# An mLSTM cell and a mixture of depths on one core: stores moved behind the loads, gates loaded later, fillers removed, gathers started sooner

## The chip, the core and the metric

The kernel runs on one core of a Trainium2 chip. The core has five engines with a queue of instructions each: TensorE (PE, matrix products), VectorE (DVE), ScalarE (ACT), GpSimd (POOL) and SyncE (SP, which only starts transfers here), and 16 DMA engines that all transfers share. Every engine works through its own queue in order and waits on semaphores for the others. The metric is the device time of one execution in microseconds. Lower is better. The kernel before takes 215.62 us, the median of 3 runs (212.85 to 220.34); the profiled execution has a span of 216.6 us.

## The reference

Two blocks follow each other. The first is an mLSTM cell for 4 batches, 8 heads, 768 positions and head size 40:

```python
for t in range(S):
    m_new  = np.maximum(f_gate[:, :, t] + m, i_gate[:, :, t])
    f_stab = np.exp(f_gate[:, :, t] + m - m_new)
    i_stab = np.exp(i_gate[:, :, t] - m_new)
    C = f_stab * C + i_stab * outer(v_t, k_t)
    n = f_stab * n + i_stab * k_t
    y[:, :, t] = sigmoid(o_gate[:, :, t]) * (C @ q_t) / max(|n . q_t|, 1)
```

The result is brought to x of shape (4, 768, 320). The second block is a mixture of depths: for each batch the scores `x @ w_gate` are ranked, the 128 highest of the 768 rows are picked, and only these get a layer:

```python
    top = argpartition(-scores[b], 128)[:128]
    h = relu(x[b, top] @ w1)              # 320 -> 1024
    out[b, top] = x[b, top] + sigmoid(scores[b, top])[:, None] * (h @ w2)
```

All other rows of the output are x itself.

## The kernel before

The recurrence is computed in blocks. One step n of the main loop (12 steps, `for n in range(N)`) handles 256 positions of one batch, all 8 heads; `b, s = divmod(n, 3)`, so each batch has the steps s = 0, 1, 2. The 256 positions are held as 128 partitions times c = 2, and the states are taken every 64 positions.

What one step does: `scores` (k times q, L260), `masked` (VectorE applies the causal mask, giving P), `update` (k times the weighted v for the next step, L227, into pU), `states` (VectorE adds up the states C), `widen` (ScalarE copies q into a padded tile), `weigh` (POOL multiplies v by the gates, giving wv, L213), `turn` (transposes of k and q on TensorE, L201, copied back by ScalarE, L203 and L205), `read` (q times the states, L282, into pH), `attend` (P times wv added into pH, L292), `divide` (VectorE normalizes, giving y, L301 to L306), `sigmoid` (ScalarE, on the output gates o), `output` (POOL multiplies y by o, giving x, L314), `store` (x to the output in DRAM), `router` (VectorE, the product of x with w_gate, L329). Update, turn, widen and weigh work ahead of their step: in step n they handle n+1 or n+2.

The second block of batch b-1 runs inside the steps of batch b: `spread` (L357, each score broadcast to all partitions; s = 0), `ranks` (each row counts the scores above its own, half of the rows on VectorE with L367, half on ScalarE by signs with L372), `select` (L404, a 0/1 matrix from ranks), `fetch` (L444, which products yield the indices of the picked rows; then POOL starts a gather from the output in DRAM, L446), `fetched` (transposes of the gathered rows, L454, and xeT on ScalarE, L456), `layer1` (L471, two halves) and `layer2` (L480, then yg on ScalarE, L485, and a scatter that adds onto the output, L486). The last batch has no gather: `picked` forms its rows by products with the selection (L428). At the end `good` says whether two assumptions held; each engine reads it into a register (L590), and a general version of the kernel, `_general`, runs only if they did not.

Order: `_fast` runs under a manual schedule, so the order of the lines of the program is the order in each engine's queue. A wait in a queue holds up everything behind it in that queue. Three tiles each (NB) hold k, q and v, four (NO) hold the output gates, two serve each use of PSUM tag "t", which turns, index products and layers share, and one holds pU, pH, and pS or pB.

Loads: `load(n + 3)` at the top of step n starts four transfers for v and k, one for q and four for o, on SyncE. The four o transfers go into the tile that `output(n - 1)` reads last. Each transfer waits for the one eight places before it to land, over SyncE's and ScalarE's transfers together, since eight semaphores serve in turn. Stores are started by ScalarE. The weights w1 and w2 are loaded in steps 1 and 2.

Fillers: `fill(k)` multiplies a tile of ones k times into a PSUM tile that nobody reads (L495), to keep TensorE at work.

Of the kernel before, what the change touches and what calls it, by code (L numbers as in the profile page):

```python
# [26 lines left out]
def _fast(ctx, tc, q, k, v, i_gate, f_gate, o_gate, w_gate, w1_in, w2_in, out):  # L27


    nc = tc.nc  # L30
# [8 lines left out]
    WARM = 14  # L39
# [19 lines left out]
    def load(n):  # L59
        if n >= N:  # L60
            return
        b, s = divmod(n, NS)
        for t, src in ((v_t, v), (k_t, k)):
            for c in range(2):
                a = s * 256 + c * 128
                SP.dma_start(out=t[n % NB][:, c, :, 0:D], in_=src[b, :, a:a + 128, :].rearrange("h p d -> p h d"))
        SP.dma_start(out=q_t[n % NB], in_=q[b, :, 256 * s:256 * s + 256, :].rearrange("h (p t) d -> p h (t d)", t=2))
        for r in range(2):
            for c in range(2):
                a = s * 256 + c * 128 + r * 64  # L70
                SP.dma_start(out=o_t[n % NO][64 * c:64 * c + 64, r], in_=o_gate[b, :, a:a + 64, :].rearrange("h p d -> p h d"))  # L71
# [19 lines left out]
    ident = const.tile([128, 128], FP, name="ident")  # L91
    for i in range(NB):
        POOL.memset(k_t[i][:, :, :, D:DP], 0.0)
        POOL.memset(v_t[i][:, :, :, D:D1], 1.0)
        if i == 0:
            make_identity(nc, ident)
        if i < 2:
            POOL.memset(qw_t[i][:, :, :, D:DP], 0.0)
        if i == 0:
            POOL.memset(wv_t[0], 0.0)  # L100
# [5 lines left out]
    ind = gate.tile([BH, 2, 64], FP, name="ind")  # L106
    DVE.tensor_copy(out=ind, in_=odd.unsqueeze(2).to_broadcast([BH, 2, 64]))
# [42 lines left out]
    def gate_rows(s):  # L150
        own = slice(256 * s, 256 * s + 256)
        carry = m[:, s:s + 1]
        F = gate.tile([BH, 256], FP, name="F", tag="F")
        a = gate.tile([BH, 256], FP, name="a", tag="a")
        M = gate.tile([BH, 256], FP, name="M", tag="M")
        Me = gate.tile([BH, 2], FP, name="Me", tag="Me")
        E = gate.tile([BH, 514], FP, name=f"E{s}")
        DVE.tensor_tensor_scan(out=F, data0=one, data1=f_sb[:, own], initial=0.0, op0=OP.mult, op1=OP.add)
        DVE.tensor_tensor(out=a, in0=i_sb[:, own], in1=F, op=OP.subtract)
        DVE.tensor_tensor_scan(out=M, data0=one, data1=a, initial=carry, op0=OP.mult, op1=OP.max)  # L160
        DVE.tensor_scalar(out=Me[:, 1:2], in0=M[:, 255:256], scalar1=-1.0, scalar2=None, op0=OP.mult)
        DVE.tensor_scalar(out=E[:, 256:512], in0=a, scalar1=M[:, 255:256], scalar2=None, op0=OP.subtract)
        DVE.tensor_tensor(out=E[:, 512:513], in0=carry, in1=M[:, 255:256], op=OP.subtract)
        DVE.tensor_scalar(out=E[:, 0:256].rearrange("b (r c t) -> b c r t", r=2, c=2),
                          in0=M.rearrange("b (c r t) -> b c r t", c=2, r=2), scalar1=M[:, 255:256], scalar2=None,
                          op0=OP.subtract)
        DVE.tensor_tensor(out=m[:, s + 1:s + 2], in0=F[:, 255:256], in1=M[:, 255:256], op=OP.add)
        ACT.activation(out=E[:, 0:513], in_=E[:, 0:513], func=AF.Exp)
        rowed[s] = E

    def gate_cols(s):
        E = rowed[s]
        dz = gate.tile([BH, 128], FP, name=f"dz{s}")
        DVE.tensor_scalar(out=dz, in0=ind.rearrange("b j e -> b (j e)"), scalar1=E[:, 512:513], scalar2=None, op0=OP.mult)
# [56 lines left out]
    def states(n):  # L231

        for i in range(4):
# [83 lines left out]
    def store(n):  # L317
        b, s = divmod(n, NS)
        for c in range(2):
            a = 256 * s + 128 * c  # L320
            ACT.dma_start(out=out[b, a:a + 128, :].rearrange("(r t) d -> t r d", t=64),
                          in_=x_t[b % 2][64 * c:64 * c + 64, 2 * s:2 * s + 2, 0:DM])
# [95 lines left out]
    def picked(b):  # L418
# [7 lines left out]
        for r in range(2 * NS):  # L426
            for j in range(3):
                PE.matmul(pX[:, j, :], x[:, r, 128 * j:128 * j + 128], sel[:, r, :],  # L428
                          start=(r == 0 and j == 0), stop=(r == 2 * NS - 1), skip_group_check=True)
        d["xeT"] = mod.tile([128, 3, 128], FP, name="xeT")  # L430
        ACT.copy(out=d["xeT"], in_=pX)
# [6 lines left out]
    def fetch(b):  # L438

        d = dep[b]  # L440
        sel = d["sel"]
        pi = ps_t.tile([128, 3], FP, name="pi", tag="t")
        for r in range(2 * NS):
            PE.matmul(pi, sel[:, r, :], place[:, r, :], start=(r == 0), stop=(r == 2 * NS - 1))  # L444
        index(b, pi[:, 0:1], pi[:, 1:2], pi[:, 2:3])
        POOL.indirect_dma_start(out=xe_t[b % 2][:, 0:DM], out_offset=None, in_=out[0:b + 1].rearrange("b s d -> (b s) d"),  # L446
                                in_offset=bass.IndirectOffsetOnAxis(ap=d["idx"], axis=0),
                                bounds_check=(b + 1) * S - 1, oob_is_err=False)
# [42 lines left out]
    def fill(k):  # L491

        pf = ps_t.tile([128, 512], FP, name="pf", tag="t")
        for i in range(k):
            PE.matmul(pf[:, 128 * (i % 4):128 * (i % 4) + 128], hot, hot, start=True, stop=True)  # L495

    gate_rows(0)
    causal()
    gate_cols(0)
    weigh(0)  # L500
    POOL.memset(wv_t[1], 0.0)
    tables()
    margins()
    turn(0, "kT")
    widen(0)
    update(0)
    turn(0, "qT")
    scores(0)
    gate_rows(1)
    gate_rows(2)  # L510
    fill(6)
    gate_cols(1)
    gate_cols(2)
    weigh(1)
    POOL.memset(wv_t[2], 0.0)
    states(0)
    for n in range(N):
# [3 lines left out]
        if n == 1:  # L521
# [3 lines left out]
        if n == 2:  # L525
            SP.dma_start(out=w2, in_=w2_in.rearrange("(f p) d -> p f d", p=128))
        if n > 0:
            scores(n)
        masked(n)
        if n < NS:  # L530
            fill(6)
        if more:
            update(n + 1)
            states(n + 1)
        sigmoid(n)
        if more:
            widen(n + 1)
        if n + 2 < N:
            weigh(n + 2)
        if n > 0:  # L540
            router(n - 1)
        if b > 0 and s == 1:
            select(b - 1)
        if more:
            turn(n + 1, "kT")
        if n < 5 or n == 7:
            fill(4)
        if b > 0 and s == 2:
            fetched(b - 1)
            layer1(b - 1, 0)  # L550
            layer1(b - 1, 4)
        if b > 1 and s == 0:
            layer2(b - 2)
        read(n)
        if more:
            turn(n + 1, "qT")
            if b > 0 and s == 0:
                dep[b - 1] = {"sb": spread(b - 1, 0, 2 * NS)}
        else:
            gated(n)  # L560
# [6 lines left out]
        if n > 0:  # L567
            store(n - 1)
        if b > 0 and s == 0:
            ranks(b - 1)  # L570
        if b > 0 and s == 1:
            fetch(b - 1)
# [3 lines left out]
    layer2(b - 1, 0, 4)  # L576
    ranks_last(b)
    store(N - 1)
    layer2(b - 1, 4)
    fill(8)  # L580
    picked(b)
    good = gate.tile([1, 1], I32, name="good")
    pg = ps_t.tile([1, NS + B], FP, name="pg", tag="t")
# [4 lines left out]
    layer1(b, 0)  # L588
    layer1(b, 4)
# [354 lines left out]
```

## Time and profile before

| what | value |
|---|---|
| median of 3 runs | 215.62 us |
| span of the profiled execution | 216.6 us |
| busy: PE, DVE, ACT, POOL | 173.7, 101.6, 73.5, 74.4 us |
| mean granted TensorE clock | 0.887 of full |
| fillers (L495), busy | 17.6 us, 112 records (each product of 32-bit numbers has two) |
| transfers | 24.33 MB, 112 GB/s over the span |

Where each step's scores begin, in us from the start of the span (TensorE's timeline, L260):

| step | 0 | 1 | 2 | 3 | 4 | 5 | 6 | 7 | 8 | 9 | 10 | 11 |
|---|---|---|---|---|---|---|---|---|---|---|---|---|
| us | 15.84 | 31.35 | 41.07 | 52.02 | 67.57 | 77.44 | 96.72 | 109.70 | 121.17 | 143.06 | 156.04 | 165.11 |

The page of the profile gives, per engine, the busy time and, in 40 slices of the span, the busy share, the clock granted to TensorE and the share of the DMA engines, each in tenths as one digit. Its chain follows the work that ended last back to what released it, and so says which engine or transfer set the end. A wait is listed with the one who waited, whom it waited for, the total, the number of times and the longest. In the tables by stage each engine has its busy time with the number of instructions in brackets, then come the clock, the DMA share and GB/s. In timelines a line is: start, length, engine, line, operation, written tile <- read tiles, sizes, count, and in square brackets the idle time before it with its releaser. "PEld" is the load of weights, "SPq" and "ACTq" are the queues that issue transfers. Busy time of an engine that nobody waits for costs nothing.

### The profile page before, as it was taken

How to read it: one execution, taken by the hardware profiler on the slowest of the kernel's cores; microseconds unless marked ns; L12 is line 12 of the kernel's file. 1: busy time of each engine (PE TensorE's matmuls, PEld its weight loads, DVE VectorE, ACT ScalarE, POOL GpSimd, SP SyncE). 2: the span in 40 equal slices, each digit the busy share in tenths (PEclk: the TensorE clock that was granted, in tenths of full speed). 3: DMA queues.
4: the chain of work that ended last, by engine and by line, in shares of the span. 5: the costliest groups of instructions: out<-in, count | busy, mean ns of one | idle time of the engine just before them, and what ended most of it. 6: DMA issues, size and time to landing. Idle time of an engine off the chain costs nothing.

```text
span 216.6 us, 6856 instructions
## 1 busy us (share of the span) xinstructions
PE 173.7 (80%) x2961; PEld 154.2 (71%) x2961; DVE 101.6 (47%) x273; ACT 73.5 (34%) x134; POOL 74.4 (34%) x95
## 2 busy tenths in 40 slices
PE   7477999899499691999997908999984299997960
PEld 7366898788499681997877808996974199696940
DVE  7795727364444974019168660056199200831000
ACT  2425141424116551143384411242592103811200
POOL 8495707070421636007243343025232500320011
PEclk9969799999959999799997975899999559998895
DMA  5999999939989789955989991020312100240002
GB/s 113 174 160 166 184 142 163 200 60 271 181 184 275 129 170 178 157 96 99 181 162 184 175 205 18 0 67 0 58 39 64 30 0 3 62 87 9 5 9 33
DMA packets 93608, 24.33 MB, mean 112 GB/s; under 512 B 88352, under 2 KB 93088, under 8 KB 93568
## 3 DMA queue, kind: packets, MB, share of 16 engines
q1 hardware_dynamic: 89392, 18.72, 51.1%
q10 hardware_dynamic: 3456, 3.93, 6.8%
q0 software_dynamic: 720, 1.15, 3.5%
q8 instruction: 25, 0.41, 0.8%
q14 instruction: 15, 0.12, 0.2%
HBM read 19.20 MB, written 4.59 MB: 110 GB/s over the span
## 4 chain that ended last, share of the span: by engine, by line
PE 45%; DMA 15%; issue 12%; SPq 7%; DVE 6%; POOL 5%; ACT 5%; ACTq 1%; POOLq 0%
PE ph L471 11%; PE pf L495 6%; DMA xe<-out_dram,idx 6%; PE pt L201 5%; SPq L71 5%; PE py L480 4%; PE pH L282 4%; PE pH L292 4%; PE pU L227 4%; DMA o<-in_o_gate_dram 3%; DMA out_dram<-x 3%; DMA v<-in_v_dram 3%; POOL wv L213 2%; PE pS L260 2%; PE pX L428 2%
## 5 line engine op out<-in xcount | busy, mean ns | idle before, releaser
L314 POOL TENSOR_TENSOR x<-y,o 128x320 f32<-128x320 f32 x24 | 20.5, 874 | 93.9 <-DVE y L306 23.3
L213 POOL TENSOR_TENSOR wv<-v,cols 64x656 f32<-64x656 f32 x24 | 31.8, 1326 | 14.3 <-DVE cols L182 5.7
L301 DVE SCALAR_TENSOR_TENSOR den<-pH,cols 128x16 f32<-128x16 f32 x12 | 2.1, 174 | 66.9 <-PE pH L292 66.9
L471 PE MATMUL ph<-xeT,w 128*128 128x128 f32 x192 | 30.7, 337 | 1.7 <-ACT xeT L456 1.7
L471 PEld LDWEIGHTS ph<-xeT,w 128*128 128x128 f32 x192 | 29.9, 251 | 2.8 <-ACT xeT L456 2.7
L205 ACT COPY qT<-pt 128x512 f32<-128x512 f32 x24 | 13.9, 629 | 26.6 <-PE pt L201 26.6
L203 ACT COPY kT<-pt 128x512 f32<-128x512 f32 x24 | 12.9, 586 | 26.8 <-PE pt L201 26.7
L227 PE MATMUL pU<-wv,k 128*64 128x82 f32 x384 | 17.8, 248 | 4.7 <-issue 2.6
L495 PE MATMUL pf<-hot 128*128 128x128 f32 x112 | 17.6, 311 | 4.5 <-ACT kT L203 4.5
L495 PEld LDWEIGHTS pf<-hot 128*128 128x128 f32 x112 | 15.4, 216 | 6.3 <-ACT kT L203 5.9
L227 PEld LDWEIGHTS pU<-wv,k 128*64 128x64 f32 x384 | 15.6, 145 | 6.1 <-issue 3.0
L480 PE MATMUL py<-w,hT 128*128 128x320 f32 x64 | 18.4, 437 | 0.6 <-ACT kT L203 0.6
L292 PE MATMUL pH<-wv,P 128*64 128x82 f32 x384 | 16.7, 239 | 0.0
L292 PEld LDWEIGHTS pH<-wv,P 128*64 128x64 f32 x384 | 14.7, 138 | 2.0 <-issue 1.3
L329 DVE CUSTOM_DVE_ANT_0 scr<-x,wg 128x320 f32<-128x320 f32 x22 | 15.2, 691 | 1.6
L239 DVE TENSOR_TENSOR C<-pU,C 128x164 f32<-128x164 f32 x40 | 13.1, 327 | 5.9 <-PE pU L227 4.8
L486 POOL DMA_INDIRECT out_dram<-yg,idx x4 | 6.3, 1584 | 27.4 <-ACT yg L485 23.7
L480 PEld LDWEIGHTS py<-w,hT 128*128 128x128 f32 x64 | 11.8, 190 | 5.4 <-ACT kT L203 1.1
L201 PE MATMUL pt<-ident,qw 128*128 128x128 f32 x96 | 15.1, 307 | 0.6 <-ACT kT L203 0.6
L260 PE MATMUL pS<-qT,kT 40*64 40x64 f32 x768 | 14.3, 221 | 1.6 <-issue 0.9
L266 DVE TENSOR_TENSOR P<-pS,mask 128x1024 f32<-128x1024 f32 x12 | 14.6, 1214 | 0.7 <-PE pS L260 0.7
L282 PEld LDWEIGHTS pH<-C,qT 40*64 40x64 f32 x704 | 13.3, 143 | 2.2 <-issue 1.3
(110 smaller groups left out, 240.6 us busy)
## 6 DMA issues: line engine op xcount, KB each, us to landing
v<-in_v_dram SPq DMA_DIRECT2D x24, 160.0 KB, 4.4
k<-in_k_dram SPq DMA_DIRECT2D x24, 160.0 KB, 4.4
q<-in_q_dram SPq DMA_DIRECT2D x12, 320.0 KB, 5.8
o<-in_o_gate_dram SPq DMA_DIRECT2D x48, 80.0 KB, 4.3
out_dram<-x ACTq DMA_DIRECT2D x24, 160.0 KB, 3.6
w<-in_moe_w_dram SPq DMA_DIRECT2D x1, 1280.0 KB
w<-in_moe_w_dram SPq DMA_DIRECT2D x2, 512.0 KB, 5.7
w<-in_moe_w_dram SPq DMA_DIRECT2D x1, 256.0 KB
```

Source lines behind the costliest of these rows:

```text
L201: PE.transpose(pt[:, p, :], src[:, c, 2 * p:2 * p + 2, :].rearrange("s j d -> s (j d)"), ident)
L213: POOL.tensor_tensor(out=wv_t[n % 3][o, :, :, r], in0=v_t[n % NB][o], op=OP.mult, in1=cols[s][o, 0:2, b * H:b * H + H].unsqueeze(3).to_bro ...
L227: PE.matmul(pU[64 * j:64 * j + 64, c, p], k_t[n % NB][:, c, 2 * p + j, :], wv_t[n % 3][:, c, 2 * p + j], start=True, stop=True)
L260: PE.matmul(pS[o, j, c, p, :], kT[e, p, t], qT[e, p, t], start=True, stop=True)
L266: DVE.tensor_tensor(out=P.rearrange(flat), in0=pending[n].pop("pS").rearrange(flat), op=OP.mult, in1=mask.unsqueeze(1).to_broadcast([128, ...
L282: PE.matmul(g["pH"][64 * c:64 * c + 64, NP * j + p, r], g["qT"][e, p, t], state[n, 2 * c + r][e, p, :], start=(c, j) not in g["begun"], st ...
L292: PE.matmul(g["pH"][64 * c:64 * c + 64, NP * j + p], g["P"][:, j, c, p, :], wv_t[n % 3][:, c, 2 * p + j], start=(c, j) not in g["begun"], ...
L314: POOL.tensor_tensor(out=x.rearrange(order, j=2, d=D), in0=pending[n]["y"][:, r].rearrange("s (j p) d -> s j p d", j=2), in1=o.rearrange(o ...
L329: DVE.tensor_tensor_reduce(out=scr, in0=x[:, r, 0:DM], in1=wg, scale=1.0, scalar=0.0, op0=OP.mult, op1=OP.add, accum_out=x[:, r, DM:DM + 1])
L471: PE.matmul(ph[:, f, :], w1[:, j, (f0 + f) * 128:(f0 + f) * 128 + 128], d["xeT"][:, j, :], start=(j == 0), stop=(j == 2))
L480: PE.matmul(d["py"], d["hT"][:, f, :], w2[:, f, :], start=(f == 0), stop=(f == NF - 1))
L495: PE.matmul(pf[:, 128 * (i % 4):128 * (i % 4) + 128], hot, hot, start=True, stop=True)
```

## The change

Five things are changed in `_fast`. Stores are started by SyncE, behind the loads of the same step, instead of by ScalarE. The output gates are loaded one step later than q, k and v. No fillers are left, and 18 instead of 14 products run at the very start. For the gathers, ranks, selection and the index products move ahead inside the s = 1 steps, and the gather stands before POOL's `output`; layer 2 of a batch moves to the s = 1 steps, where it runs before the update, and layer 1 behind the turn of q. In the tail the layers of the last two batches follow each other: the third batch's rows, its layer 1 (in halves, with the ranking of the last batch between) and layer 2, then the last batch's. The start is rearranged as well: most zeroing moves from POOL to ScalarE, the gate rows are split in two, and the gates of steps 1 and 2 are computed in step order, one each in the start and in step 0. The purpose is to let TensorE go on with useful work, to let loads run ahead of TensorE and to have the gathered rows there when layer 1 wants them.

```diff
-    WARM = 14
+    WARM = 18
     def load(n):
...
+        if n < N:
+            b, s = divmod(n, NS)
...
+        n -= 1
+        if 0 <= n < N:
...
+                SP.dma_start(out=o_t[n % NO][64 * c:64 * c + 64, r],
+                                 in_=o_gate[b, :, a:a + 64, :].rearrange("h p d -> p h d"))
...
+    def zero(t):
+        shape = [128, 2, H, t.shape[-1]]
+        ACT.activation(out=t, in_=hot[:, 0:1].unsqueeze(2).unsqueeze(3).to_broadcast(shape), func=AF.Copy, scale=0.0)
...
     def store(n):
...
-            ACT.dma_start(out=out[b, a:a + 128, :].rearrange("(r t) d -> t r d", t=64),
+            SP.dma_start(out=out[b, a:a + 128, :].rearrange("(r t) d -> t r d", t=64),
...
     def picked(b):
-        for r in range(2 * NS):
-            for j in range(3):
-                PE.matmul(pX[:, j, :], x[:, r, 128 * j:128 * j + 128], sel[:, r, :],
-                          start=(r == 0 and j == 0), stop=(r == 2 * NS - 1), skip_group_check=True)
-        ACT.copy(out=d["xeT"], in_=pX)
+        for j in range(3):
+            for r in range(2 * NS):
+                PE.matmul(pX[:, j, :], x[:, r, 128 * j:128 * j + 128], sel[:, r, :], start=(r == 0), stop=(r == 2 * NS - 1))
+            ACT.copy(out=d["xeT"][:, j], in_=pX[:, j])
...
+    gate_sums(0)
     gate_rows(0)
+    gate_sums(1)
     causal()
     gate_cols(0)
     weigh(0)
...
     turn(0, "kT")
+    gate_rows(1)
     widen(0)
     update(0)
     turn(0, "qT")
+    gate_cols(1)
+    weigh(1)
+    gate_sums(2)
     scores(0)
-    gate_rows(1)
-    gate_rows(2)
-    fill(6)
-    gate_cols(1)
-    gate_cols(2)
-    weigh(1)
-    states(0)
     for n in range(N):
         load(n + 3)
-        if n == 1:
+        if n == 3:
 ...
-        if n == 2:
+        if n == 4:
 ...
         if n > 0:
+            store(n - 1)
+        if n > 0:
             scores(n)
         masked(n)
-        if n < NS:
-            fill(6)
+        if n == 0:
+            states(0)
+            gate_rows(2)
+        if b > 1 and s == 1:
+            layer2(b - 2)
+        if n > 0 and (s < 2 or not more):
+            router(n - 1)
+        if b > 0 and s == 1:
+            ranks(b - 1)
+            select(b - 1)
         if more:
             update(n + 1)
-            states(n + 1)
-        sigmoid(n)
-        if more:
+            states(n + 1, 0, 4 if n else 3)
             widen(n + 1)
...
-        if n < 5 or n == 7:
-            fill(4)
-        if b > 0 and s == 2:
-            fetched(b - 1)
-            layer1(b - 1, 0)
-            layer1(b - 1, 4)
-        if b > 1 and s == 0:
-            layer2(b - 2)
         read(n)
+        if b > 0 and s == 1:
+            numbers(b - 1)
+            fetch(b - 1)
+        if n == 0:
+            gate_cols(2)
+            states(1, 3)
+            weigh(2)
+            tables()
         if more:
             turn(n + 1, "qT")
+            sigmoid(n)
             if b > 0 and s == 0:
                 dep[b - 1] = {"sb": spread(b - 1, 0, 2 * NS)}
+            if b > 0 and s == 2:
+                fetched(b - 1)
+                layer1(b - 1, 0)
+                layer1(b - 1, 4)
...
-        if n > 0:
-            store(n - 1)
-        if b > 0 and s == 0:
-            ranks(b - 1)
-        if b > 0 and s == 1:
-            fetch(b - 1)
...
     output(N - 1)
-    layer2(b - 1, 0, 4)
+    fetched(b - 1)
+    layer1(b - 1, 0)
     ranks_last(b)
     store(N - 1)
-    layer2(b - 1, 4)
-    fill(8)
+    layer1(b - 1, 4)
+    layer2(b - 1)
     picked(b)
     layer1(b, 0)
     layer1(b, 4)
+    picked_numbers(b)
     layer2(b)
```

`numbers` is the first half of what `fetch` was (the index products and VectorE's arithmetic on them), `picked_numbers` the last lines of what `picked` was.

## The prediction

> **What bounds the kernel now.** I read the page's slices first (its rows for the granted TensorE clock and for the DMA), then its chain, then the table of waits, the busy time by stage, and TensorE's timeline. A "step" n below is one block of 256 rows, and begins when its scores (L260) begin.
>
> ```profile
> PEclk9969799999959999799997975899999559998895
> DMA  5999999939989789955989991020312100240002
> ```
>
> One slice is 5.4 us. The DMA engines are full until slice 23 (about 126 us) and nearly idle afterwards; the matmul clock is low in some six places. So two thirds of the kernel run beside a full DMA, and the last third has none to blame.
>
> ```profile
> PE 45%; DMA 15%; issue 12%; SPq 7%; DVE 6%; POOL 5%; ACT 5%; ACTq 1%; POOLq 0%
> ```
>
> The chain is mostly TensorE. What stops it (who waits <- for whom: us in total, times, longest), with the load queue's own waits in the last two lines:
>
> ```profile
> PE pX L454 <- DMA xe<-out_dram,idx: 14.9, 3, 5.3
> SPq L71 <- DMA out_dram<-x: 12.0, 3, 7.1
> SPq L66 <- DMA out_dram<-x: 12.0, 4, 6.6
> ```
>
> Three gathers of picked rows cost TensorE 14.9 us, and loads on SyncE wait 24 us behind stores. By stage (steps 1 and 5 of 0 to 11):
>
> ```profile
> 31.40:41.10 9.70, 9.46 (x234) 8.51 (x232) 5.48 (x12) 2.93 (x6) 4.22 (x4) 1.00 1.10 165
> 77.40:96.70 19.30, 14.34 (x264) 13.29 (x260) 5.89 (x20) 5.35 (x10) 5.84 (x5) 0.91 0.90 155
> ```
>
> In step 1 TensorE is busy 9.46 of 9.70 us, but 2.7 of that are fillers; in step 5 it is idle 5 us. The timeline shows both kinds of loss:
>
> ```profile
> 32.44 1.60 PE L495 MATMUL pf<-hot 128*128 128x128 f32 x12
> 56.71 0.64 PE L227 MATMUL pU<-wv,k 128*64 128x82 f32 x11 [2.61 <-issue]
> 62.54 1.97 PE L201 MATMUL pt<-ident,qw 128*128 128x128 f32 x8
> 85.31 0.52 PE L454 MATMUL pX<-ident,xe 128*128 128x128 f32 x3 [4.39 <-DMA xe<-out_dram,idx]
> 86.39 7.00 PE L471 MATMUL ph<-xeT,w 128*128 128x128 f32 x48 [0.57 <-ACT xeT L456]
> ```
>
> The transposes of 62.54 take 1.97 us where others take 1.09: half clock, after the gap of 2.61 us.
>
> [...]loads move at 165 GB/s while slices with weights reach 271.
>
> **Prices**, start to start at full clock: scores 1.1, update 1.3, k turn 1.05, read 1.07, q turn 1.03, attend 1.3: a plain step needs 6.8 us of TensorE. The score broadcast (L357) adds 1.4, layer 1 7.0, layer 2 4.5.
>
> **Part by part.**
>
> Costed at nothing: the 18 instead of 14 warming products lie in the wait for the first gates (TensorE idles 1.6 us before 7.46); the constants made later on POOL stand beside TensorE's turns; the picked rows copied in thirds save 0.2 us, in the tail's sum.
>
> Fillers out: 56 products, 17.6 us busy, nearly all in line on TensorE. They lie in the start and in steps 0 to 4 and 7 (about 15 us) and in the tail (1.9, partly beside the ranking).
>
> Start: the zeroing goes to ScalarE[...] the first gates are ready at 5.4, since the 2.5 us of "ind" are gone: nothing lost, scores(0) at 14.8 instead of 15.8. Step 0 held 15.5 us: both further gate rows, a DVE-to-PE round trip, two fillers. In the new order only gates 2 stand in it: 6.8 + 0.8 of transposes + about 2 of waiting for POOL's wv(1) (2.6 us after cols(1)) = 9.7.
>
> Output gates later: each load set is 0.98 MB of q, k, v, then 0.33 MB of gates of the step before. They need not wait for output(n-1) (POOL), and k, v, q arrive 2 us sooner. At 165 GB/s, with 1.2 us per pair of stores and about 4.4 us each for w1 and w2 (their slices run at 271 GB/s), set n has landed at about 16, 23, 31, 39, 48, 57, 69, 83, 92, 101, 110 us (n = 1 to 11; each is the one before plus 1.31 MB at 165 GB/s = 7.9 us, plus the 1.2 us of the stores from set 5 on, plus 4.4 us for w1 ahead of set 7 and w2 ahead of set 8). TensorE needs set n+1 at 1.1 us into step n. By the sums below it arrives just in time for steps 1 to 4, and early afterwards.
>
> Stores behind loads: ScalarE loses 24 issues of 0.62 us, 1.2 us a step, which lay beside TensorE: nothing gained directly. A store now waits on SyncE for output(n-1), 3.5 us into step n; behind it stand the loads of n+4, whose buffers come free only about 4 us into step n: no loss. But store(2) stands behind load 6, gates 5 and w1, so it lands near 65 us, and the first gather needs it.
>
> Steps with s=1 (4, 7, 10): ranks, selection and indices are pulled up. VectorE: mask until 2.95 us after the step's start, router until 4.1 (POOL's second x), three comparisons of 1.07, selection 0.95: 8.4. TensorE reaches the index product (L444 of before) at 4.5 and stands for 3.9 us; the second q turn then waits for its PSUM buffer until VectorE has made the states (1.4) and the indices (0.5), 10.4. Step 4 takes 12.2 us against 7.05 of work. In steps 7 and 10 layer 2 (4.5) fills that hole, but its ScalarE output stands ahead of the three sign passes (3.3 us), so selection ends at 10.6: 14.4 us.
>
> Steps with s=2 (5, 8): indices were ready 11.7 us into step 4, now 10.4, and layer 1 moves behind the q turn, 5.5 us into the next step. From index to landed rows took 6.0 us in step 4 of before (79.3 to 85.3), of which 1.7 waited for POOL's multiplication (L314), behind which the gather no longer stands; about 4.5 is left, and the rows are there: the stalls of 4.4, 5.3 and 5.2 us go. Left is 1.5 us for sigmoid and xeT copy. 6.8 + 0.5 + 7.0 + 1.5 = 15.8. Step 5 alone waits for store(2): rows at 69 us, TensorE there at 65: +4.2.
>
> Steps with s=0 (3, 6, 9): 8.5 (6.8 + 1.4 + gaps). Layer 2 leaves 6 and 9.
>
> Sum: 14.8 start; 9.7, 7.2, 7.5, 8.5, 12.2, 20.0, 8.5, 14.4, 15.8, 8.5, 14.4 = 126.7 for steps 0 to 10 (before: 149.3).
>
> Tail from scores(11): scores, read, broadcast after router(10), attend 6.4; transposes 0.6; xeT behind four sign passes 2.9; layer 1 in halves with the broadcast of the last rows 7.6; layer 2 4.5; picked rows 4.3 and last copy 0.3; layer 1 7.0; then index product, indices, flags, "good" and its register load (0.48 us, now between layers on TensorE) 2.3; layer 2 4.5; scatter to the end as before 7.3: 47.8 (before 51.5).
>
> 14.8 + 126.7 + 47.8 = 189. This is at full clock with no issue gaps. Before, TensorE's busy 173.7 us stands against 162.6 by my prices, so 11 us went to the low clock, in five or six places; the new order also has five gaps of 1.8 us or more. I add 10: **199 us**. With half of that and no store wait: 190.
>
> **Rivals.** (a) The transfers eat the gain: stores queue behind loads at each batch, gathers stall three times by 5 us, sets arrive late. 199 + 12 = 211. For it: DMA near 1.0 until 126 us, so the floor for the last set is 110 to 118. Against: after step 5 TensorE needs longer per step than the 9 us of DMA. (b) No change: the waits in s=1 steps are 5 us longer than I think and the clock falls in each: 199 + 3 x 6 = 217. (c) Slower: without fillers TensorE works 6.8 of 8 us in the early steps with gaps after every turn; if the clock stays halved in steps 0 to 4 (34 us of work, +17) and in the three s=1 steps (+8), 224. Against: steps 9 and 10 of before ran without fillers at 1.00 with gaps of 0.57 and 1.28 us.
>
> **Chances.** Mine 0.68, (a) 0.13, (b) 0.10, (c) 0.09. Faster by over 2% means below 211.3: mine, most of (a): 0.79; same 0.11; slower 0.10. The range leaves out some of (b) and all of (c), and on the low side a case without clock losses: 187 to 215.
>
> **What would show it.** No fillers and steps 1 to 3 at 7 to 8 us; DMA share near 1 up to about 110 us; no wait of layer 1 for the gather in steps 8 and 11, some in step 5; a TensorE wait for the selection of about 4 us in step 4 and 2 us in 7 and 10. The prediction fails if the clock row shows fives through the early steps, if set n+1 is waited for at each update, or if the s=1 steps exceed 15 us.

## The result and the profile after

The changed kernel takes 197.5 us, the median of 4 runs (194.79 to 200.07), against 215.69 for the kernel before in the same comparison: ratio 0.912, 95% interval 0.892 to 0.933. The forecast was 199.0 us with a range of 187 to 215. The profiled execution has a span of 196.1 us and took 198.05. Because single runs of one program lie up to 8% apart (the kernel before from 205 to 222 us over all comparisons), each ratio here and below, and each time that an experiment gives ahead of its brackets, is taken over the runs within 1.5% of the fastest of their kernel in that comparison; the brackets behind a time hold the range of all runs, those behind a ratio its 95% interval, and a ratio is always to the kernel before, run beside it. A later comparison of the same two kernels gave a ratio of 0.942 (0.933 to 0.951), 194.75 against 206.87 us. So the gain is real, and its size lies between some 5 and 11%.

The page: the granted clock and the DMA share in 40 slices, of 4.9 us each now, and the chain by engine.

```profile
PEclk9975589999996698599999699999988979999996
DMA  5999999859788978998799889720221202020002
PE 57%; issue 9%; ACT 9%; DMA 8%; DVE 7%; SPq 4%; POOL 2%; POOLq 0%; ACTq 0%; DVEq 0%
```

TensorE's part of the chain went from 45% to 57%, and DMA and the load queue from 22% to 12%. The DMA engines are busy until the 26th slice (about 127 us; before, until the 24th, about 130), so the transfers end about when they did; what ends sooner is the work after them. The clock is lowest in the fourth and fifth slice (14.7 to 24.5 us, step 0) and in the 17th (78 to 83 us, step 5 after its wait), and reduced in the 13th and 14th (step 4), the 23rd (step 7) and the 33rd (the tail after its wait).

The waits: first TensorE's longest, then the longest of SyncE's transfers.

```profile
PE pi L456 <- DVE sel L415: 7.3, 3, 4.2
PE pX L470 <- DMA xe<-out_dram,idx: 4.9, 1, 4.9
PE pU L238 <- issue: 4.2, 1, 4.2
PE ph L487 <- ACT xeT L472: 4.2, 3, 2.7
SPq L332 <- POOL x L325: 30.5, 5, 13.8
```

The wait for gathered rows fell from 14.9 us in three places to 4.9 in one. In exchange TensorE waits for the selection, 7.3 us. Loads no longer wait for stores; the stores wait 30.5 us for the rows they store, and TensorE waits for none of the loads that stand behind them in the queue.

By stage, with the columns named ahead of the prediction (steps 0, 1 and 5, and the tail from the scores of step 11):

```profile
16.00:30.50 14.50, 10.18 (x200) 9.11 (x199) 10.61 (x28) 4.21 (x7) 4.94 (x4) 0.66 1.03 170
30.50:37.30 6.80, 6.80 (x213) 6.16 (x211) 5.96 (x12) 4.77 (x8) 6.41 (x17) 1.00 0.89 145
67.00:88.50 21.50, 15.73 (x267) 14.37 (x263) 7.09 (x16) 5.20 (x10) 6.04 (x5) 0.84 0.97 206
149.30:196.10 46.80, 32.73 (x345) 28.09 (x343) 13.01 (x40) 10.78 (x28) 9.10 (x8) 0.93 0.13 24
```

Step 1 is nothing but useful TensorE work at full clock: 6.80 of 6.80 us. Steps 0 and 5 are two of the places where TensorE still idles beside a full DMA; step 4, with its 4.2 us for the selection, is the third.

TensorE's timeline at its waits:

```profile
22.23 2.46 PE L238 MATMUL pU<-wv,k 128*64 128x82 f32 x32 [4.23 <-issue]
61.73 0.32 PE L456 MATMUL pi<-place,sel 128*128 128x3 bf16 x6 [4.21 <-DVE sel L415]
78.06 0.87 PE L470 MATMUL pX<-ident,xe 128*128 128x128 f32 x3 [4.89 <-DMA xe<-out_dram,idx]
79.50 7.74 PE L487 MATMUL ph<-xeT,w 128*128 128x128 f32 x48 [0.57 <-ACT xeT L472]
107.16 0.30 PE L456 MATMUL pi<-place,sel 128*128 128x3 bf16 x6 [1.54 <-DVE sel L415]
119.10 5.62 PE L487 MATMUL ph<-xeT,w 128*128 128x128 f32 x48 [0.96 <-ACT xeT L472]
159.14 4.52 PE L487 MATMUL ph<-xeT,w 128*128 128x128 f32 x24 [2.66 <-ACT xeT L472]
184.24 4.54 PE L496 MATMUL py<-w,hT 128*128 128x320 f32 x16 [0.96 <-DVE good L607]
```

The two layers 1 at 79.50 and 119.10 are the same 48 products: 7.74 us after a wait of 4.89, 5.62 after one of 0.96. The half layer of 159.14 took 4.52 where half of 5.62 would do.

Lengths of the steps, from one scores to the next, in one trace each (executions of 218.44 us before and 198.05 after):

| | start | 0 | 1 | 2 | 3 | 4 | 5 | 6 | 7 | 8 | 9 | 10 | tail |
|---|---|---|---|---|---|---|---|---|---|---|---|---|---|
| before | 15.8 | 15.5 | 9.7 | 11.0 | 15.6 | 9.9 | 19.3 | 13.0 | 11.5 | 21.9 | 13.0 | 9.1 | 51.5 |
| forecast | 14.8 | 9.7 | 7.2 | 7.5 | 8.5 | 12.2 | 20.0 | 8.5 | 14.4 | 15.8 | 8.5 | 14.4 | 47.8 |
| after | 16.0 | 14.5 | 6.8 | 6.8 | 8.9 | 14.1 | 21.4 | 8.1 | 15.2 | 14.2 | 8.1 | 15.2 | 46.8 |

### The profile page after: what moved, and what is told of

Read it like the earlier page. It is cut to its first block, busy times and chain, and to the rows that moved or that the text cites. A ratio compares the mean times of both kernels' runs of the same rounds, so it can differ in the third digit from the quotient of the medians.

```text
span 196.1 us, 6660 instructions
## 1 busy us (share of the span) xinstructions
PE 157.8 (80%) x2857; PEld 138.3 (71%) x2857; DVE 106.2 (54%) x269; ACT 77.9 (40%) x142; POOL 72.0 (37%) x89
## 4 chain that ended last, share of the span: by engine, by line
PE 57%; issue 9%; ACT 9%; DMA 8%; DVE 7%; SPq 4%; POOL 2%; POOLq 0%; ACTq 0%; DVEq 0%
PE ph L487 13%; PE pt L212 9%; PE py L496 7%; PE pH L303 7%; PE pU L238 5%; PE pS L271 4%; ACT sgn L383 4%; DMA v<-in_v_dram 4%; PE pH L293 3%; PE warm L89 3%; DMA xe<-out_dram,idx 3%; PE pX L440 2%; PE pB L368 2%; DMA o<-in_o_gate_dram 2%; POOL wv L224 1%
## 5 line engine op out<-in xcount | busy, mean ns | idle before, releaser
L224 POOL TENSOR_TENSOR wv<-v,cols 64x656 f32<-64x656 f32 x24 | 34.3, 1428 | 25.7 <-DVE cols L193 19.6
L487 PE MATMUL ph<-xeT,w 128*128 128x128 f32 x192 | 26.4, 304 | 4.2 <-ACT xeT L472 4.2
L487 PEld LDWEIGHTS ph<-xeT,w 128*128 128x128 f32 x192 | 25.6, 218 | 5.2 <-ACT xeT L472 5.1
L340 DVE CUSTOM_DVE_ANT_0 scr<-x,wg 128x320 f32<-128x320 f32 x22 | 22.4, 1018 | 4.7 <-POOL x L325 3.0
L216 ACT COPY qT<-pt 128x512 f32<-128x512 f32 x24 | 14.2, 628 | 21.3 <-PE pt L212 21.2
L238 PEld LDWEIGHTS pU<-wv,k 128*64 128x64 f32 x384 | 15.6, 146 | 8.9 <-issue 5.3
L303 PE MATMUL pH<-wv,P 128*64 128x82 f32 x384 | 18.8, 258 | 0.0
L303 PEld LDWEIGHTS pH<-wv,P 128*64 128x64 f32 x384 | 16.8, 155 | 2.2 <-issue 1.5
L212 PE MATMUL pt<-ident,qw 128*128 128x128 f32 x96 | 16.9, 322 | 1.8 <-DVE flags L426 0.7
L496 PEld LDWEIGHTS py<-w,hT 128*128 128x128 f32 x64 | 11.8, 190 | 5.6 <-issue 1.0
L212 PEld LDWEIGHTS pt<-ident,qw 128*128 128x128 f32 x96 | 12.1, 161 | 3.9 <-PE pt L212 1.7
L271 PE MATMUL pS<-qT,kT 40*64 40x64 f32 x768 | 14.8, 229 | 0.0
L293 PE MATMUL pH<-C,qT 40*64 40x41 f32 x704 | 13.9, 229 | 0.9 <-DVE y L317 0.6
L277 DVE TENSOR_TENSOR P<-pS,mask 128x1024 f32<-128x1024 f32 x12 | 14.6, 1213 | 0.0
L293 PEld LDWEIGHTS pH<-C,qT 40*64 40x64 f32 x704 | 12.4, 134 | 3.0 <-issue 2.3
L250 DVE TENSOR_TENSOR C<-pU,C 128x164 f32<-128x164 f32 x40 | 13.1, 326 | 1.9 <-PE pU L238 0.8
```

The costliest lines, as they stand in the source:

```text
L212: PE.transpose(pt[:, p, :], src[:, c, 2 * p:2 * p + 2, :].rearrange("s j d -> s (j d)"), ident)
L216: ACT.copy(out=T.rearrange("e p (u t) -> e t p u", t=2)[:, c], in_=pt)
L224: POOL.tensor_tensor(out=wv_t[n % 3][o, :, :, r], in0=v_t[n % NB][o], op=OP.mult, in1=cols[s][o, 0:2, b * H:b * H + H].unsqueeze(3).to_bro ...
L238: PE.matmul(pU[64 * j:64 * j + 64, c, p], k_t[n % NB][:, c, 2 * p + j, :], wv_t[n % 3][:, c, 2 * p + j], start=True, stop=True)
L271: PE.matmul(pS[o, j, c, p, :], kT[e, p, t], qT[e, p, t], start=True, stop=True)
L277: DVE.tensor_tensor(out=P.rearrange(flat), in0=pending[n].pop("pS").rearrange(flat), op=OP.mult, in1=mask.unsqueeze(1).to_broadcast([128, ...
```

## The experiments

### The fillers, in the new order and in the old

In the new order: the changed kernel with the 56 filler products at their old places.

```diff
+    scores(0); fill(6)
...
+        if n < NS:
+            fill(6)
...
+        if n < 5 or n == 7:
+            fill(4)
...
+    fill(8)
```

> The changed kernel with the 56 filler products put back where the kernel before has them. My theory: they stand in line on TensorE, so nearly all of their time comes back in the steps where TensorE has no wait (1 to 3, with 2.7 us each), and less where they fall into a hole (steps 0 and 4): 197.5 + 8 to 13 = 206 to 211 us. Rival: they only fill waits and keep the clock up (0.66 and 0.76 in steps 0 and 4 of the changed kernel), so that they cost nothing or even help: 194 to 199 us.

Measured: 208.84 us (206.56 to 212.45), ratio 0.993 (0.985 to 1.000). Against the changed kernel's 195.87 in the first comparison, taken the same way, some 13 us come back, and next to nothing of the gain is left. Steps 1, 2 and 3 take 9.7, 10.1 and 9.9 us instead of 6.8, 6.8 and 8.9, at a mean clock of 1.00, which step 1 has without fillers too (6.80 above): there they are plain work in line and keep no clock that would be lost. Step 0 takes 15.0 instead of 14.5 with 16 of the fillers in it, at a mean clock of 0.87 instead of 0.66. There the rival was right in part: the clock gives back most of what they cost.

In the old order: the kernel before with the same lines taken out and nothing else.

> The kernel before with nothing changed but the fillers taken out. My theory: 10 to 14 us of the 17.6 are in line and go: 202 to 206 us (ratio 0.94 to 0.955). Rival: its steps are paced by transfers (DMA near full until 126 us), so TensorE merely waits instead, and its clock falls: 212 to 217 us (ratio 0.985 or more).

Measured: 206.48 us (205.38 to 208.57) against 209.76, ratio 0.985 (0.977 to 0.992): 3.3 us, far less of a gain than I expected, and a ratio at the edge of the rival's. The waits of this kernel show where the time went:

```profile
PE pX L454 <- DMA xe<-out_dram,idx: 11.8, 3, 5.2
PE pU L227 <- POOL wv L213: 10.1, 3, 5.3
```

The rows are still waited for (11.8 us), and TensorE, ahead sooner, now waits 10.1 us for POOL's products of v (2.0 in the kernel before). Step 0 is no shorter without its fillers, 15.6 us at a mean clock of 0.67 against 15.5 at 0.89. Taking the fillers out of the old order brings 1.5%, the rest of the change with the fillers left in 0.7%, and both together 6 to 9%. The parts bring more than their sum. I read it so that each takes away work or a wait in which the other's gain would be lost; the runs show the sum, not this reason. No run keeps fillers in step 0 alone.

### Stores on ScalarE again

The changed kernel, with the stores issued by ScalarE at the end of the step as before.

```diff
-            SP.dma_start(out=out[b, a:a + 128, :]...
+            ACT.dma_start(out=out[b, a:a + 128, :]...
...
-        if n > 0:
-            store(n - 1)
...
             output(n)
+        if n > 0:
+            store(n - 1)
```

> The changed kernel with the stores started by ScalarE again, at the end of each step. My theory: store(2) no longer stands behind load 6 and w1, so the 4.9 us wait for the first gather in step 5 goes; ScalarE's 1.2 us of issuing per step lie beside TensorE except in the s=1 steps: 193 to 198 us. Rival: the move to SyncE is what lets the loads run ahead, since loads no longer wait for stores of another queue (24 us of waits in the kernel before): then 202 us or more.

Measured: 192.51 us in one run and 195.64 to 198.94 in the other five, so no loss, and the rival's 202 is not reached. Loads wait for stores again:

```profile
SPq L531 <- DMA out_dram<-x: 7.8, 1, 7.8
SPq L67 <- DMA out_dram<-x: 5.0, 1, 5.0
SPq L74 <- DMA out_dram<-x: 4.7, 2, 3.2
```

That is 17.5 us of waits on the load queue, and the time does not show them: the sets arrive early enough all the same. Step 5 lost its wait for the rows and took 17.0 instead of 21.4 us, as the first theory said. But the tail took 50.9 instead of 46.8, with more of it at half clock (a mean clock of 0.83 from 149.3 to 196.1 us, against 0.93 there in the changed kernel), its last layer in part:

```profile
146.00 1.99 PE L271 MATMUL pS<-qT,kT 40*64 40x64 f32 x64
183.00 6.20 PE L496 MATMUL py<-w,hT 128*128 128x320 f32 x16 [0.95 <-DVE good L607]
```

(1.16 and 4.54 at full clock.) The mean clock of this trace, 0.86, is the lowest of all that I have, and how much of that belongs to the edit stays open. Shown is that the gain does not need the stores on SyncE.

### Output gates with their own set again

```diff
     def load(n):
...
-        n -= 1
-        if 0 <= n < N:
-            b, s = divmod(n, NS)
             for r in range(2):
```

> The changed kernel with the output gates loaded together with q, k and v of the same step. My theory: each set comes 2 us later while the DMA is the pace in steps 1 to 4, and a set again waits on SyncE for POOL's output of the step before: 2 to 6 us more, 200 to 203 us. Rival: TensorE has slack to the transfers everywhere (steps 1 to 3 of the changed kernel wait for nothing), so no difference: 197 to 198.5 us.

Measured: 197.5 us (196.5 to 204.16), ratio 0.943 (0.933 to 0.952), against 0.942 for the changed kernel. The rival was right: no difference is shown, and TensorE waits for no load in either kernel.

### The second block in the old order

The changed kernel with router, ranks, selection, index products, layer 1 and layer 2 at the old places inside the steps and in the tail.

```diff
-        if b > 1 and s == 1:
-            layer2(b - 2)
...
-            ranks(b - 1)
-            select(b - 1)
...
+        if b > 0 and s == 1:
+            select(b - 1)
...
+        if b > 0 and s == 2:
+            fetched(b - 1)
+            layer1(b - 1, 0)
+            layer1(b - 1, 4)
+        if b > 1 and s == 0:
+            layer2(b - 2)
         read(n)
...
+        if b > 0 and s == 0:
+            ranks(b - 1)
+        if b > 0 and s == 1:
+            numbers(b - 1)
+            fetch(b - 1)
```

> The changed kernel (stores on SyncE, later gates, no fillers, new start) with the second block in the order of the kernel before: ranks at the end of s=0 steps, indices and gather at the end of s=1 steps, layer 1 ahead of read, layer 2 in s=0 steps, and the old tail. My theory: the three waits for gathered rows come back (4 to 5 us each) and the s=1 steps get shorter by 4 to 6 us, as in the kernel before without fillers, whose steps 3 to 10 took 110.5 us and tail 50.8 against 105.2 and 46.8: 204 to 208 us. Rival: what was gained beside the fillers comes from the loads and the start, and the order of the second block moves waits only: 197 to 200 us.

With it ran the changed kernel once more, as the measure of this comparison:

> The changed kernel as it is, beside the next three on the same chip, as their reference. Both theories: 196 to 199 us.

Measured: 206.82 us (204.32 to 209.7), ratio 0.992 (0.985 to 0.998), against 194.75 (194.5 to 200.96) and 0.942. The old order costs 12.1 us; without the new one, all else that was changed, the fillers included, is worth under 2%. Its waits name the main reason:

```profile
PE pX L470 <- DMA xe<-out_dram,idx: 19.2, 3, 9.1
PE pi L456 <- DVE sel L415: 5.3, 3, 2.4
```

19.2 us for the rows, 4.3 more than in the kernel before. The surplus lies in step 5, 9.05 us against 4.39. Missing fillers don't explain it, since the kernel before without fillers has 11.8 us; store(2), which stands behind loads and w1 on SyncE here too, would, but no run tests that in the old order. In the changed order it was 4.9, and 3.2 in the second trace of the same program: there the gather starts 0.6 us later, but step 5 begins 1.7 us later, and TensorE has less left to wait.

### Index products after attend

The selection is waited for at L456. This kernel puts `numbers` and `fetch` behind `attend`, so that TensorE has its own products meanwhile.

```diff
         read(n)
-        if b > 0 and s == 1:
-            numbers(b - 1)
-            fetch(b - 1)
...
         attend(n)
+        if b > 0 and s == 1:
+            numbers(b - 1)
+            fetch(b - 1)
```

> The changed kernel with the index products and the gather after attend in the s=1 steps, so that TensorE turns q and attends while VectorE ranks. My theory: step 4 falls from 14.1 to about 9.5 us, but step 5 then waits longer for the same gather, which store(2) holds until 69.5 us; steps 7 and 10 lose 2 us each: 192 to 195 us. Rival: TensorE then waits at the product's new place for as long, and the gather is late: 197 to 201 us.

Measured: 194.55 us (194.41 to 197.34), against 194.75: no difference that the scatter lets me see. The waits moved:

```profile
PE pX L470 <- DMA xe<-out_dram,idx: 7.3, 2, 6.6
PE pi L456 <- DVE sel L415: 2.4, 1, 2.4
```

The selection cost 7.3 us and now costs 2.4; the rows cost 4.9 and now 7.3. Of 4.9 us, 2.4 came back as another wait.

### store(2) ahead of the loads of step 6

```diff
+        if n == 3:
+            store(n - 1)
         load(n + 3)
...
-        if n > 0:
+        if n > 0 and n != 3:
             store(n - 1)
```

> The changed kernel with one edit: at step 3 the store of rows 2 is issued ahead of the loads of step 6 and of w1, and nothing else moves. Theory (the 4.9 us wait for gathered rows in step 5 comes of the store that lands late behind those loads): the gather starts by about 67 instead of 72 us, the wait in step 5 falls from 4.9 us to under 1.5, step 5 from 21.4 to about 17.5, and the time is 192 to 195 us. Rival (the waiting TensorE only moves: the loads of step 6 land later, or the shorter idle time is lost to a halved clock, as it was with the stores on ScalarE): step 5 is shorter, but a later step or the tail is longer by as much, and the time is 195.5 to 198.

Measured: 195.45 us (194.21 to 198.92), ratio 0.939 (0.928 to 0.951). The mechanism is as the theory said: the gather starts at 65.4 instead of 72.0 us and nobody waits for its rows. First POOL's gather in this kernel, then in the changed one:

```profile
65.36 1.25 POOL L462 DMA_INDIRECT xe<-out_dram,idx  x1 [3.39 <-issue]
```

```profile
72.01 1.25 POOL L462 DMA_INDIRECT xe<-out_dram,idx  x1 [11.96 <-DVE C L258]
```

Step 5 takes 16.9 us, against 21.4 and 20.3 in the two traces of the changed kernel. Step 4 takes 15.0 instead of 14.1, with 5.1 us of wait for the selection, but this is no cost of the edit: the second trace of the changed kernel has 15.2 and 5.3. The ratio shows no gain against 0.942; where step 5's saving goes is not shown. The change had put w1 in front of store(2) as well: its diff moves the loads of w1 and w2 from steps 1 and 2 to 3 and 4, which the list of five changes leaves out, and no run moves them back.

### The hole in step 0

TensorE's 4.23 us before 22.23 are put down to "issue", that is to nothing that the profile shows. The other engines at that time, in the changed kernel:

```profile
16.48 2.91 POOL L224 TENSOR_TENSOR wv<-v,cols 64x656 f32<-64x656 f32 x2 [5.13 <-DVE cols L193]
16.54 1.76 DVE L162 TENSOR_TENSOR_SCAN F<-one,f_sb 32x256 f32<-32x256 f32 x1
18.34 1.33 DVE L163 TENSOR_TENSOR a<-i_sb,F 32x256 f32<-32x256 f32 x1
19.60 1.21 DVE L277 TENSOR_TENSOR P<-pS,mask 128x1024 f32<-128x1024 f32 x1
21.07 1.05 DVE L250 TENSOR_TENSOR C<-pU,C 128x164 f32<-128x164 f32 x3
```

wv for the second update is there at 19.39. But pU has one PSUM buffer, VectorE reads the first update out of it last at 22.12 (21.07 + 1.05), and TensorE starts at 22.23. The next kernel moves the two instructions that stand ahead on VectorE.

```diff
     weigh(1)
-    gate_sums(2)
     scores(0)
...
             states(0)
+            gate_sums(2)
             gate_rows(2)
```

> The changed kernel with one line moved: gate_sums(2), the scan F and the difference a of the third set, is emitted after states(0) instead of ahead of scores(0). Theory (the 4.2 us that TensorE loses ahead of the second update in step 0 is no gap of its own: pU has one PSUM buffer, and VectorE reads the first update out of it only after the scan and the difference, 3.1 us beside GpSimd's multiplications): the wait falls to about 1.5 us, the second update starts once wv is there, step 0 takes 11.5 to 12.5 instead of 14.5 us, and the time falls by 2 to 3, to 192.5 to 195. Rival (a gap of TensorE's own, as the profile's word for it says): step 0 stays at 14.5 us and the time at 195.5 to 198.

Measured: 195.18 us (194.13 to 199.16), ratio 0.937 (0.929 to 0.945), between the two ranges.

```profile
17.04 1.23 DVE L277 TENSOR_TENSOR P<-pS,mask 128x1024 f32<-128x1024 f32 x1 [0.69 <-PE pS L271]
18.53 1.05 DVE L250 TENSOR_TENSOR C<-pU,C 128x164 f32<-128x164 f32 x3
19.69 2.45 PE L238 MATMUL pU<-wv,k 128*64 128x82 f32 x32 [2.79 <-POOL wv L224]
19.87 0.67 DVE L162 TENSOR_TENSOR_SCAN F<-one,f_sb 32x256 f32<-32x256 f32 x1
31.09 1.81 PE L271 MATMUL pS<-qT,kT 40*64 40x64 f32 x64
```

The cause is shown: the read ends at 19.58, and TensorE starts at 19.69, again 0.11 us behind it. The gap fell from 4.23 to 2.79 us (I had expected 1.5), and the update starts 3.95 us after the scores instead of 6.21. The gain is not there: step 0 takes 15.4 us. All of its products from 19.69 to 31 run at half clock, where in the changed kernel the clock was back at about 26 (and had been halved before the gap already: its scores took 1.99, here 1.16). Both of my theories missed that; the step is short of clock as well as held up. The edit alone does not decide when the clock comes back: two kernels below have the same instructions in step 0 and the same gap of 2.79 us, and it is back at 26.3 us in one (step 0: 13.7 us) and at 33.8 in the other (16.2 us). This trace has no wait for rows in step 5 either: step 5 begins at 69.2 instead of 67.1 and the gather at 70.0 instead of 72.0. So the absence of that wait in one trace proves nothing for an edit; for store(2) ahead the early start of the gather does.

### All repairs together

First the late index products, store(2) ahead, layer 2 behind ranks and selection, and in the tail the sign passes behind the copy xeT.

```diff
-        if b > 1 and s == 1:
-            layer2(b - 2)
...
             select(b - 1)
+        if b > 1 and s == 1:
+            layer2(b - 2)
...
-            ranks_first(b)
...
     fetched(b - 1)
+    ranks_first(b)
     layer1(b - 1, 0)
```

> The changed kernel with four moves: index products and gather after attend; store(2) ahead of load 6 and w1; layer 2 emitted after ranks, so that ScalarE makes the signs before layer 2's output; in the tail the four sign passes after the copy of the gathered rows. My theory: step 4 loses 4.7 us, the gather wait in step 5 4 to 5, steps 7 and 10 3 to 4 each, the tail 2.7: 180 to 186 us. Rival: in steps 4 to 6 the transfers set the pace (sets 7 and 8 with w1 and w2), and what TensorE gains there it waits for loads: 189 to 193 us.

Measured: 188.27 us (187.92 to 192.66), ratio 0.909 (0.900 to 0.918), 6.5 us below the 194.75 beside it, between the two theories. Steps 7 and 10 fell from 15.2 to 11.5 each, step 4 from 14.1 to 9.5, while steps 6 and 8 grew by 1.3 and 1.1. Left are 2.4 us for the selection and 3.9 for rows, since the late index products make the gather late. The tail did not get its 2.7 us: the wait for xeT fell from 2.66 to 0.57, but the half layer behind it runs at half clock (4.91 us, against 2.84 for the other half), and the tail takes 47.5 us against 46.8. Layer 2 behind the ranks and the late sign passes did not run alone. With only the index products late, steps 7 and 10 took 13.1 and 14.6 us, so 4.6 us of what these two steps lost comes with the other moves, most likely with layer 2.

Then gate_sums(2) late as well:

> The kernel of the four repairs (numbers after attend, store 2 ahead, layer 2 after the ranks, tail signs after the copy; 188.5 us) with gate_sums(2) moved after states(0) as well. Theory: what step 0 loses stands ahead of everything else, so that nothing later takes it back: 185 to 187 us. Rival: the loads set the pace of steps 1 to 4 (transfers near full), and what step 0 gives is waited for there: 187.5 to 189.5.

Measured: 186.88 us (185.87 to 191.27), ratio 0.892 (0.881 to 0.903). This is inside the theory's range, but the interval overlaps that of the kernel of four repairs, so a gain is not shown. The rival's reason does not hold: TensorE waits for no load. The gap before the second update fell to 2.79 us, and step 0 took 13.7 instead of 14.7, with its first half at half clock again (scores 1.99, update 2.45).

Then the gathered rows and layer 1 behind attend:

```diff
-            if b > 0 and s == 2:
-                fetched(b - 1)
-                layer1(b - 1, 0)
-                layer1(b - 1, 4)
         attend(n)
+        if b > 0 and s == 2 and more:
+            fetched(b - 1)
+            layer1(b - 1, 0)
+            layer1(b - 1, 4)
```

> The kernel of the run before (four repairs and gate_sums(2) late), with the gathered rows and layer 1 of a batch emitted after attend of the third step instead of ahead of it. Theory (what is left of the wait for gathered rows, 2.9 and 0.9 us, is hidden by attend's 1.4 to 2.7 us of products): steps 5 and 8 together 2 to 3 us shorter, time 183 to 186. Rival (attend's divisions and outputs then run beside layer 1 instead of after it, but attend itself waits for VectorE's product with the mask, which layer 1 hid until now): a wait for P takes the place of the wait for rows, and the time stays within 1 us of the run before.

Measured: 184.56 us (183.83 to 192.33), ratio 0.884 (0.873 to 0.895). Its longest waits:

```profile
PE pU L238 <- POOL wv L224: 3.5, 3, 2.1
PE pU L238 <- issue: 2.8, 1, 2.8
PE pi L456 <- DVE sel L415: 2.8, 1, 2.8
PE ph L487 <- ACT xeT L472: 1.7, 3, 0.6
```

No wait for gathered rows is left, and none for P came in its place. Steps 5 and 8 take 16.1 and 14.4 us against 19.8 and 16.4 in the run before, 5.7 less together; the time fell by 2.3, and step 0 of this profile took 2.4 us longer at half clock. This version is some 10 us faster than the changed kernel (0.884 against 0.942; 194.75 us, in a neighbouring comparison on another chip).

## Why the prediction was right

**The mechanism held, the closeness is in part luck.** Fillers out, gathers sooner, stores harmless: the forecast 199.0, the time 197.5. Start, steps and tail came to 189 by my sum and to 16.0 + 133.2 + 46.8 = 196.0 in the trace. Of the table above, the terms that were too small lack 11.3 us together (step 0 alone 4.8) and those that were too large have 4.5 too much (step 8 alone 1.6). The lump of 10 us, which I guessed and did not work out, covered the difference of 7. My sum was also of the span, and the time of an execution is some 2 us longer (198.05 for 196.1), which it left out. Nor did I see that fillers and order depend on each other: I put some 15 us on the fillers, and out of the old order alone they brought 3.3.

**Step 0, "9.7", took 14.5.** The step's "about 2 of waiting for POOL's wv(1)" was the wrong wait. It was 4.23 us, for VectorE, which had to empty pU's single buffer first; I had followed wv and not the buffer. The rest is half clock: scores 1.99 instead of 1.1, update 2.46 instead of 1.3, k turn 1.72 instead of 1.05. And VectorE itself was slow: the scan F took 1.76 us while POOL multiplied wv (16.48 to 19.39), and 0.67 us in the kernel where it came after. The product with the mask took about the same either way, 1.21 us without POOL beside it and 1.23 with it in that other kernel. What makes the scan slow and leaves the product as it is, no run shows.

**Layer 1, "7.0", takes 5.62** at full clock (119.10 above). I read 7.00 off the kernel before, where three of the four layers 1 stood behind a wait of 4 to 5 us for rows and ran partly at half clock (a mean of 0.79 over those 7.00 us, and 7.00 x 0.79 is 5.5). So the price held a piece of the stall that I was removing. That explains 1.4 of the 1.6 us in step 8, 14.2 instead of 15.8.

**Step 4 and steps 7, 10.** The wait for the selection in step 4 was 4.21 us (3.9 predicted) and 1.54 in 7 and 10 ("2 us"). Steps 7 and 10 took 15.2 instead of 14.4, step 4 14.1 instead of 12.2, at a mean clock of 0.76: the gap of 4.2 us was paid again after it. By my own sign of failure, an s = 1 step over 15 us, this part failed narrowly in two of three steps. One cost I had not seen: the router products overlap POOL's multiplications now. The group in the kernel before and after (busy us, mean ns):

```profile
L329 DVE CUSTOM_DVE_ANT_0 scr<-x,wg 128x320 f32<-128x320 f32 x22 | 15.2, 691 | 1.6
```

```profile
L340 DVE CUSTOM_DVE_ANT_0 scr<-x,wg 128x320 f32<-128x320 f32 x22 | 22.4, 1018 | 4.7 <-POOL x L325 3.0
```

The same 22 instructions, 7.2 us more: 0.48 to 0.49 us without POOL beside them, mostly 1.13 to 1.6 with it. Only 0.65 us of it falls into each of steps 4, 7 and 10, ahead of their comparisons; of the rest, TensorE's waits show 0.9 us, in the tail.

**Step 5, "20.0", took 21.4.** The working was right in its wait: store(2) behind the loads, rows late, 4.89 us against 4.2. Issuing it first removes that wait. Layer 1 behind it took 7.74, and not the 5.62 of full clock.

**Steps 8 and 11, no wait for rows: right.** Two of the three stalls of about 5 us are gone, and the third is the one in step 5; the old order in the changed kernel makes them 19.2 us.

**The tail, "47.8", took 46.8.** The wait of xeT behind the sign passes was 2.66 (2.9 in the sum), the register load 0.96 of 2.4 from the last layer 1 to the last layer 2 (2.3 in the sum).

**Costed at nothing.** Stores and their queue: no loss found with them back on ScalarE. Zeroing: ScalarE is done with what it has to do before the first gates (two writes of 128 x 1312 at 1.29 and 1.28 us, two of 128 x 384 at 0.51 each) at 5.41 us and then waits 0.24 us for VectorE. The later output gates were worth 2 us sooner arrival in my working and nothing that the ratios show (0.943 and 0.942), since the sets were early anyway. The warming products were not free. ScalarE has the first gates ready at 6.28 us, a us sooner than before, but TensorE is at warming products and begins the gate products at 7.39 without a pause (7.46 before). The second group of these, whose input is there at 7.04, starts at 7.67, and POOL's wv and the first update hang on it. That is up to 0.6 of the 1.2 us that the start took over its 14.8; half clock from 12.3 us on has a part in the rest. No run has fewer warming products, so this is read from the trace and not shown.

**The rivals.** (a), transfers eat the gain, fell: DMA is busy until 127 us (I had said about 110) and TensorE waits for no load. (b) was right that the s = 1 steps take longer than I thought, by 0.8 to 1.9 us each instead of 6. (c) fell where it mattered: steps 1 to 3 run at 1.00 without a single filler. But steps 0 and 4 ran at 0.66 and 0.76, and its price was too low: 34 us of work at half clock would cost not 17 but, as I estimate from scores of 1.99 for 1.16 and an update of 2.46 for 1.35, some 24 to 28 us. Two slips in the sums change nothing: the landing of set 7 by its own rule is 70.5 and not 69, and the tail's terms add up to 47.7.

What stays open: why the clock in step 0 comes back at 26 us in one trace and at 33 or 34 in another, even with the same instructions, what the new start is worth by itself, and how much of the tail's half clock with the stores on ScalarE belongs to that edit.

## What to carry to other kernels

A price taken from a trace holds the state it was measured in: take it from an instance over which the clock was full (layer 1: 5.62 us, against 7.00 behind a wait), or a stall is counted both in the wait and in the work. When a TensorE wait has no releaser in the profile, look at who last reads the PSUM buffer it is to write; that reader's queue may be what sets the time (here the read ended at 22.12 us and TensorE started at 22.23). Judge an edit that hides one wait by the list of waits and not by the median alone: here three single repairs took 1.4 to 4.9 us out of one wait each and gained nothing measurable, and four together gained 6.5 us, six some 10. Part of that is a move that never ran alone, so it does not show that repairs gain only together. Fillers and the order around them are to be judged together: taking out the fillers alone brought 1.5%, the rest of the change alone 0.7, both 6 to 9.

## What the hardware showed that I had not expected

Two VectorE operations took longer beside GpSimd's multiplications: the scan of 32 x 256 1.76 us instead of 0.67, the difference after it 1.33 instead of 0.41. The 128 x 320 products with accumulation went from 0.49 to between 1.13 and 1.6 us in most such places.

The granted clock of TensorE changed on a grid. In the clock records of the traces before and after (18 and 14 stretches), every stretch at half or full clock, but for the last of each, is a whole multiple of 3.41 us, from 3.41 to 34.13; around step 0 of the changed kernel it is 13.65 us at half, then 34.13 at full, then 6.83 at half. When the clock came back after a gap was not a function of the gap's length alone: after 4.23 us idle it was back 3.7 us of work later, after 2.79 us idle 5.3, 12.5 and 12.9 us later in three traces with the same instructions in step 0. What sets the 3.41 us, and why the clock came back so late in two of the three, no run here explains.
